# Batch 0's attention masks move from TensorE to VectorE, the mask table becomes the second transfer, and the planner gets step durations read from a trace

## The chip, the core and the metric

The kernel runs on one core of one Trainium2 chip. The metric is the device time of one execution in microseconds, lower is better. Before the change the median of three runs is 916.32 us (913.51 to 917.98).

A core has five engines, each with its own in-order queue: TensorE (PE, matmuls, with PEld for its weight loads), VectorE (DVE), ScalarE (ACT), GpSimd (POOL) and SyncE (SP), which here only issues transfers. An instruction at the head of a queue that waits holds everything behind it on that engine.

## What is computed

Attention with two kinds of sliding window, followed by a feed-forward layer with a rational activation. The masks are the part that the change is about:

```python
scores = scale * np.matmul(q, k.transpose(0, 1, 3, 2))      # 8 batches, 8 heads, 576 positions, 64 wide
mask_plain = (rel >= 0) & (rel < window)                     # window 32
mask_dil = (rel >= 0) & (rel < window * dilation) & (rel % dilation == 0)   # dilation 4
scores = np.where(masks[None, :, :, :], scores, -1000000000.0)
attn = softmax(scores)                                       # max, exp, sum, division
x = matmul(attn, v)                                          # 4608 tokens of 512
h = x @ w_in                                                 # 512 -> 2048
P = a[0] + a[1] * h + a[2] * h2 + a[3] * h3
Q = 1.0 + np.abs(b[0]) * np.abs(h) + np.abs(b[1]) * h2
out = (P / (Q + 1e-06)) @ w_out                              # 2048 -> 512
```

Heads 0 to 3 use the plain window, heads 4 to 7 the dilated one; the tokens of the dilated heads are reordered on the host so that their window is also 32 neighbours.

## The kernel before

**Attention in units.** Each batch has six units (class `Unit`). A unit is one 128 x 384 block of scores in PSUM (two banks of 192 columns), held as 32 queries by 64 keys, so each score block covers the whole window of its queries. The steps of a unit are planned in `Unit.plan` (L509): load queries and keys in one 448 KB transfer (`load_qk`), load the values in 384 KB (`load_v`), scores (`scores`, 48 small matmuls), mask, row maximum, subtraction, exponential, sum, reciprocal (VectorE and ScalarE), scaling by the reciprocal (GpSimd, `norm`), a transposition, the product with the values (`av`) and the split of the result into a high and a low part (`evac_hi`, `evac_lo`), which together are the tokens `x` of that batch. For batches 0 and 1 the transposition is done by TensorE; for the others by VectorE with a trip through DRAM. Leftover tokens (positions 512 to 575) are put aside in DRAM (`put_left`).

**The masks.** The table `mask_t` has six 64-column blocks of zeros and -1e30 in bf16, loaded once (96 KB, L903). Units of batches 0 and 1 (`on_pe`, L260) have them added by TensorE: `scores` first multiplies an identity with the mask blocks into the two banks (two matmuls of 192 columns), and then accumulates the scores on top. The scores therefore wait for the mask table and for the identity that GpSimd makes. Units of the other batches have them added by VectorE in place after the scores (`mask`, L291): one or two `tensor_tensor` instructions, by the unit's entry in `MASK_AT`. Units 0, 4 and 5 have two pieces of 192 columns, units 1 to 3 one of 384.

**The feed-forward layer in tiles.** A tile (class `Tile`) is 512 tokens by 128 of the 2048 hidden features. There are 144: nine token groups by 16 feature blocks, in the order group 0 blocks 0 to 7, group 1 all 16, group 0 blocks 8 to 15, and then groups 2 to 8. A tile is 12 matmuls into a bank (`h`), twelve steps of the activation on ScalarE, VectorE and GpSimd, and 12 matmuls into the four output banks (`out`). Group b needs the six units of batch b; the ninth group is the leftovers. The 12 matmuls come from splitting every fp32 number into a high and a low part and taking three products.

**The weights.** 32 blocks of 512 KB (16 `wi`, 16 `wo`) are loaded and each is split on the chip (`plan_weights`, L689): scaled and shifted words (ScalarE, or ScalarE or GpSimd), joined (VectorE), a high part (any of three) and a low part (VectorE or GpSimd).

**What sets the order.** Nothing is ordered by hand. A planner (class `Plan`) runs on the host while the program is built: it simulates the engines with the durations written beside every step, always taking, among steps that can start soonest on an engine, the one of the lowest rank, and emits the instructions in that order. Where a step may run on several engines, it also picks the engine. The constants that steer it:

- the cost of each step, in nanoseconds (`op({"DVE": 470}, ...)`), and the model of transfers (`DMA_START`, `DMA_NS`, `DMA_RATE`, L86);
- `DUE`: for each batch, when its last unit is due (in tiles) and the distance between its units;
- `LATE`: for each step of a tile from the 36th on, its rank beside its tile's number;
- `SLACK`: how far ahead of need scores, loads and weights (`wi`, `wo`) are ranked. For the first 36 tiles and for attention the rank of a step is worked back from the steps that need it (`Plan.due`, L106): the rank of the next step, less the cost, less the slack.

The loads of batch 0 and of the weights are chained in the order of their ranks (L980). Extra order is given with `follows`: here L909, where the mask table follows the six coefficients of the activation (`lc`). All transfers are issued by SyncE from one queue through `load` (L208). Matmuls are issued through `mm` (L211), VectorE's two-operand instructions through `tt` (L217) and `stt` (L220), GpSimd's through `ptt` (L223), ScalarE's through `act` (L214); the profile's lines are mostly those of these helpers, so tiles are named by their tensors: `pair`, `pair_A`, `pair_B` are attention's PSUM banks, `h` and `out` those of the tiles, `mx` the maxima, `p` the exponentials, `a`, `r`, `t`, `gh`, `gl` the activation's, `wi_raw` a loaded weight block, `left<-l` a store of leftovers.

Of the kernel before, what the change touches and what calls it, by code (L numbers as in the profile page):

```python
# [13 lines left out]
AF = mybir.ActivationFunctionType  # L14
# [27 lines left out]
LOG_SHIFT = 40  # L42
# [36 lines left out]
class Plan:  # L79
# [6 lines left out]
    DMA_START, DMA_NS, DMA_RATE = 3300.0, 1750.0, 375.0  # L86
# [97 lines left out]
def tile_attention_moe(  # L184
# [72 lines left out]
    class Unit:  # L257
        def __init__(self, b, u):
            self.b, self.u, self.n = b, u, b * NU + u
            self.start, self.on_pe, self.by_pe = b == 0, b < ON_PE, b < BY_PE  # L260
# [248 lines left out]
        def plan(self, by, tags):  # L509
# [20 lines left out]
            if kind == 2:  # L530
                mx = op({"DVE": 470}, 0, lambda e: self.max(True), ma)
                sb = op({"PE": 760}, 0, lambda e: self.sub_pe(), mx, identity)
                su = ex = op({"ACT": 480}, 0, lambda e: self.exp_s(), sb)
                sm = op({"DVE": 470}, 0, lambda e: self.sum(), ex)
# [3 lines left out]
            else:  # L538
                mx = op({"DVE": 470}, 0, lambda e: self.max(), ma)
                su = op({"DVE": 500}, 0, lambda e: self.sub(), mx)  # L540
                ex = op({"ACT": 425}, 0, lambda e: self.exp(), su)
                sm = op({"DVE": 470}, 0, lambda e: self.sum(), ex)
# [36 lines left out]
            if start:  # L579
                av = op({"PE": 1500}, 0, lambda e: self.av(), *self.placed, lv)  # L580
# [5 lines left out]
        def finish(self, av):  # L586
# [10 lines left out]
            low = {"DVE": sum(120 + 2 * c[1] / 0.96 for c, _ in main)}  # L597
            kl = lf = None
            if start:
                ms = eh  # L600
                if LESS[u]:
                    ms = op({"PE": sum(60 + 2 * c[1] / 1.6 for c, _ in main)}, 0, lambda e: self.less_hi(), eh, identity)
# [8 lines left out]
            else:  # L611
                low["POOL"] = sum(100 + 2 * c[1] / 0.49 for c, _ in main)
# [305 lines left out]
    for key in keys:  # L918
        plan_weights(key)
# [127 lines left out]
```

## Time and profile before

| | before |
|---|---|
| median of three runs | 916.32 us (913.51 to 917.98) |
| profiled execution | 916.49 us |
| its span in the profile | 914.7 us |
| TensorE busy | 883.2 us (97%) |
| VectorE busy | 742.3 us (81%) |
| ScalarE busy | 675.4 us (74%) |
| GpSimd busy | 467.7 us (51%) |
| mean granted TensorE clock | 0.994 of full |
| bytes moved by transfers | 103.46 MB, mean 113 GB/s |

The profile is of one execution; its own time is 916.49 us, 1.8 us more than the span from its first to its last instruction. Busy time says how long an engine was executing, not that it sets the end: TensorE's busy share is the highest, so the idle time of TensorE, stage by stage, is what can be won. "Releaser" is what ended a wait. A time to landing is from the issue of a transfer to its completion.

### The profile page before, as it was taken

Reading aid. Unit: us, or ns where it says so; the run is one execution under the profiler, and the core shown is the slowest. Engines: PE = TensorE matmul, PEld = TensorE weight load, DVE = VectorE, ACT = ScalarE, POOL = GpSimd, SP = SyncE. Lnnn points to the kernel's source line nnn. Section 1 sums busy time; section 2 is a strip of 40 time slices with the busy share of each in tenths; the row PEclk is TensorE's granted clock in tenths of the full one; section 3 lists DMA queues with packets and bytes.
Section 4 is the critical chain, followed back from the end, with each engine's and each line's share of the span. In section 5 each row is a group of like instructions: output and inputs, shape, how many; then the busy total and the mean of one; then the engine's idle time right before and its main releaser. Section 6 shows DMA issues by size and latency. Waiting matters only on the chain.

```text
span 914.7 us, 21129 instructions
## 1 busy us (share of the span) xinstructions
PE 883.2 (97%) x8153; PEld 716.1 (78%) x8153; DVE 742.3 (81%) x1312; ACT 675.4 (74%) x1092; POOL 467.7 (51%) x408
## 2 busy tenths in 40 slices
PE   5877999999999999999999999999999999999998
PEld 3755787887877878888888888888888788888876
DVE  4789999999988988788978888887779677566656
ACT  2676888877666777877787778677777688778764
POOL 2454554656635554555455555546455545444442
PEclk9989999999999999999999999999999999999999
DMA  9667460235633343334334324423333220001001
GB/s 359 240 221 249 154 234 1 99 124 190 198 99 110 110 134 118 119 111 125 115 113 127 121 83 146 129 82 85 115 95 91 61 69 1 1 1 47 0 1 47
DMA packets 85477, 103.46 MB, mean 113 GB/s; under 512 B 37376, under 2 KB 62848, under 8 KB 85376
## 3 DMA queue, kind: packets, MB, share of 16 engines
q1 hardware_dynamic: 85376, 102.11, 34.5%
q8 instruction: 64, 1.05, 0.5%
q14 instruction: 37, 0.30, 0.1%
HBM read 75.21 MB, written 26.87 MB: 112 GB/s over the span
## 4 chain that ended last, share of the span: by engine, by line
PE 75%; DVE 11%; DMA 5%; ACT 5%; issue 3%; POOL 1%; SPq 1%; DVEq 0%; POOLq 0%; ACTq 0%
PE out L212 34%; PE h L212 34%; PE pair L212 5%; DVE h L221 3%; DVE a L221 2%; DMA wi_raw<-in_w_in_dram 2%; ACT r L215 2%; DVE t L218 1%; DVE a L218 1%; DVE gl L218 1%; DMA wo_raw<-in_w_out_dram 1%; SPq L209 1%; DMA qk<-in_qk_dram 1%; ACT a L215 1%; PE pair_B L212 1%
## 5 line engine op out<-in xcount | busy, mean ns | idle before, releaser
L212 PE MATMUL h<-xh,wi 128*128 128x512 f32 x1136 | 378.1, 394 | 6.8 <-DVE a L221 6.5
L212 PE MATMUL out<-gh,wo 128*128 128x512 f32 x1136 | 353.8, 393 | 0.7 <-DVE os L218 0.7
L224 POOL TENSOR_TENSOR a<-r,a 128x512 f32<-128x512 f32 x121 | 156.6, 1294 | 241.1 <-ACT r L215 233.4
L212 PEld LDWEIGHTS h<-xh,wi 128*128 128x128 f32 x1136 | 214.5, 189 | 58.3 <-DVE a L221 12.6
L212 PEld LDWEIGHTS out<-gh,wo 128*128 128x128 f32 x1136 | 211.2, 188 | 45.9 <-DVE os L218 1.1
L212 PE MATMUL out<-gl,wo 128*128 128x512 f32 x568 | 221.8, 391 | 1.6 <-DVE gl L218 1.0
L212 PE MATMUL h<-xl,wi 128*128 128x512 f32 x568 | 222.4, 391 | 0.0
L224 POOL TENSOR_TENSOR gl<-a,gh 128x512 fp32r<-128x512 f32 x129 | 175.1, 1357 | 64.7 <-ACT gh L215 64.0
L221 DVE SCALAR_TENSOR_TENSOR h<-h,na_t,r 128x512 f32<-128x512 f32 x142 | 106.9, 753 | 111.0 <-ACT r L215 109.2
L215 ACT ACTIVATE r<-a,ln_bias 128x512 f32<-128x512 f32 x141 | 101.9, 723 | 82.8 <-POOL a L224 80.3
L215 ACT ACTIVATE r<-a,ab_t 128x512 f32<-128x512 f32 x141 | 114.7, 814 | 16.3 <-DVE a L221 14.5
L212 PEld LDWEIGHTS out<-gl,wo 128*128 128x128 f32 x568 | 106.6, 188 | 25.6 <-POOL gl L224 1.5
L212 PEld LDWEIGHTS h<-xl,wi 128*128 128x128 f32 x568 | 107.3, 189 | 21.5
L215 ACT ACTIVATE a<-h 128x512 f32<-128x512 f32 x140 | 83.5, 596 | 53.7 <-PE h L212 35.0
L215 ACT ACTIVATE t<-h,na_t 128x512 f32<-128x512 f32 x142 | 109.6, 772 | 5.0 <-PE h L212 4.6
L221 DVE SCALAR_TENSOR_TENSOR h<-t,na_t,h 128x512 f32<-128x512 f32 x142 | 107.3, 756 | 4.9
L215 ACT ACTIVATE r<-r,exp_bias 128x512 f32<-128x512 f32 x144 | 104.3, 724 | 4.7
L218 DVE TENSOR_TENSOR t<-t,h 128x512 f32<-128x512 f32 x142 | 96.6, 681 | 7.2 <-ACT t L215 7.1
L221 DVE SCALAR_TENSOR_TENSOR a<-a,r 128x512 f32<-128x512 f32 x141 | 100.2, 711 | 0.0
L221 DVE SCALAR_TENSOR_TENSOR a<-a,h 128x512 f32<-128x512 f32 x140 | 96.2, 687 | 4.8
L215 ACT ACTIVATE gh<-a 128x512 fp32r<-128x512 f32 x130 | 81.5, 627 | 23.2 <-PE out L212 14.9
L224 POOL TENSOR_TENSOR p<-p,sm 128x384 f32<-128x384 f32 x48 | 47.7, 993 | 34.3 <-DVE sm L352 28.1
(115 smaller groups left out, 712.4 us busy)
## 6 DMA issues: line engine op xcount, KB each, us to landing
qk<-in_qk_dram SPq DMA_DIRECT2D x48, 448.0 KB, 5.0
v<-in_vp_dram SPq DMA_DIRECT2D x48, 384.0 KB, 3.7
out_dram<-os SPq DMA_DIRECT2D x36, 256.0 KB, 2.3
wi_raw<-in_w_in_dram SPq DMA_DIRECT2D x16, 512.0 KB, 6.1
wo_raw<-in_w_out_dram SPq DMA_DIRECT2D x16, 512.0 KB, 6.9
results<-y SPq DMA_DIRECT2D x42, 192.0 KB, 2.4
z<-results SPq DMA_DIRECT2D x168, 48.0 KB, 2.5
turned<-u SPq DMA_DIRECT2D x36, 192.0 KB, 2.0
```

The costliest lines, as they stand in the source:

```text
L209: pin(nc.sync.dma_start(dst, src))
L212: pin(nc.tensor.matmul(o, lhs, rhs, start=start, stop=stop, skip_group_check=free))
L215: pin(nc.scalar.activation(o, i, func, **kw))
L218: pin(nc.vector.tensor_tensor(o, x, y, op))
L221: pin(nc.vector.scalar_tensor_tensor(o, x, s, y, op0, op1))
L224: pin(nc.gpsimd.tensor_tensor(o, x, y, op))
```

## The change

VectorE adds the masks of batch 0 after the scores, as it already does for batches 2 to 7; only batch 1 is left on TensorE. The mask table's load now follows the first load of unit 0 (its queries and keys), and the coefficients, unit 0's values and unit 1's queries follow the mask table. The coefficients no longer go ahead of the mask. The planner's costs are replaced by others, most of them higher, its model of transfers starts earlier (1000 instead of 3300 ns), and `DUE`, `LATE` and `SLACK` have other values, so that the order of instructions on all engines can differ everywhere.

```diff
-DUE = [(-41.16, 11.47), (-146.25, 19.43), (423.68, 72.57), (61.95, 5.87), (470.95, -17.55), (494.47, -17.25), (93.76, -24.29), (711.56, 21.96)]
+DUE = [(-42.07, 2.46), (-139.34, 32.05), (537.93, 65.82), (48.88, 1.36), (612.07, -16.51), (466.6, 3.64), (193.6, -47.08), (642.51, 32.87)]
-LATE = {"ab": -187.16, "ql": -342.11, "pl": -25.5, "qq": -118.36, "t1": -2.55, "t2": -120.77, "ln": 177.41, "ex": -496.7, "g0": -73.65, "g1": -54.63, "g2": -312.0, "gh": -189.38, "gl": 379.92, "out": 3.83}
-SLACK = {"sc": 2.49, "qk0": -51.8, "v0": -50.12, "load": 7.26, "wi": 11.43, "wo": -2.45, "w": -16.22, "gl": -5.19, "out": -6.13}
+LATE = {"ab": -175.8, "ql": -427.82, "pl": 40.09, "qq": -63.71, "t1": -55.04, "t2": 2.39, "ln": 298.24, "ex": -490.51, "g0": -123.79, "g1": -68.03, "g2": -457.35, "gh": -55.8, "gl": 283.1, "out": 3.9}
+SLACK = {"sc": 2.19, "qk0": -56.0, "v0": -56.99, "load": -3.78, "wi": 3.42, "wo": -2.73, "w": -16.4, "gl": -6.19, "out": -2.25}
...
-    DMA_START, DMA_NS, DMA_RATE = 3300.0, 1750.0, 375.0
+    DMA_START, DMA_NS, DMA_RATE = 1000.0, 1700.0, 380.0
...
-            self.start, self.on_pe, self.by_pe = b == 0, b < ON_PE, b < BY_PE
+            self.start, self.on_pe, self.by_pe = b == 0, b == 1, b < BY_PE
...
-                sc = op({"PE": 1320 + 300 * self.on_pe}, 0, lambda e: (prev.av(), self.scores()), *prev.placed, prev.lv, lq, *masks)
+                sc = op({"PE": 1320 + 700 * self.on_pe}, 0, lambda e: (prev.av(), self.scores()), *prev.placed, prev.lv, lq, *masks)
...
-                sc = op({"PE": 1130 + 320 * self.on_pe}, 0, lambda e: self.scores(), lq, *masks)
+                sc = op({"PE": 1500 + 450 * self.on_pe}, 0, lambda e: self.scores(), lq, *masks)
...
-            no = op({"POOL": 790}, 0, lambda e: self.norm(e), rc)
+            no = op({"POOL": 880}, 0, lambda e: self.norm(e), rc)
...
-                tr = op({"PE": 690}, 0, lambda e: self.transposes(), no, identity)
+                tr = op({"PE": 900 if start else 600}, 0, lambda e: self.transposes(), no, identity)
...
-                av = op({"PE": 1500}, 0, lambda e: self.av(), *self.placed, lv)
+                av = op({"PE": 2000}, 0, lambda e: self.av(), *self.placed, lv)
...
-            jn = op({"DVE": 680}, 0, lambda e: w_join(key), sc, lw, lock=True)
+            jn = op({"DVE": 710}, 0, lambda e: w_join(key), sc, lw, lock=True)
...
-        lo = op({"DVE": 602, "POOL": 1280}, 0, lambda e: w_lo(key, e), hi, lock=True)
+        lo = op({"DVE": 625, "POOL": 1350}, 0, lambda e: w_lo(key, e), hi, lock=True)
...
-    lc = op({"SP": 60}, -39.5, lambda e: load(coef_t, coef), dma=3000)
-    masked.follows.append(lc)
+    lc = op({"SP": 430}, -39.3, lambda e: load(coef_t, coef), dma=3000)
...
+    masked.follows.append(first_loads[0])
+    for o in (lc, *first_loads[1:3]):
+        o.follows.append(masked)
```

Some more costs change in the same way, nearly all upwards (the sum goes from 470 to 510, the logarithm from 615 to 660; the transposition of batch 1 goes from 690 to 600).

More of the change, by code (lines that the diff above doesn't have):

```diff
@@ L531, in plan @@
                 mx = op({"DVE": 470}, 0, lambda e: self.max(True), ma)
-                sb = op({"PE": 760}, 0, lambda e: self.sub_pe(), mx, identity)
+                sb = op({"PE": 950}, 0, lambda e: self.sub_pe(), mx, identity)
                 su = ex = op({"ACT": 480}, 0, lambda e: self.exp_s(), sb)
-                sm = op({"DVE": 470}, 0, lambda e: self.sum(), ex)
+                sm = op({"DVE": 510}, 0, lambda e: self.sum(), ex)
             elif kind:
@@ L540, in plan @@
                 su = op({"DVE": 500}, 0, lambda e: self.sub(), mx)
-                ex = op({"ACT": 425}, 0, lambda e: self.exp(), su)
-                sm = op({"DVE": 470}, 0, lambda e: self.sum(), ex)
+                ex = op({"ACT": 470}, 0, lambda e: self.exp(), su)
+                sm = op({"DVE": 510}, 0, lambda e: self.sum(), ex)
             rc = op({"DVE": 300}, 0, lambda e: self.recip(), sm)
-            no = op({"POOL": 790}, 0, lambda e: self.norm(e), rc)
+            no = op({"POOL": 880}, 0, lambda e: self.norm(e), rc)
             if self.by_pe:
-                tr = op({"PE": 690}, 0, lambda e: self.transposes(), no, identity)
+                tr = op({"PE": 900 if start else 600}, 0, lambda e: self.transposes(), no, identity)
                 pl = op(BOTH, 0, lambda e: self.place(e), tr)
@@ L596, in finish @@
             eh = op({"ACT": sum(172 + 2 * c[1] / 1.4 * 0.75 for c, _ in main)}, 0, lambda e: self.evac_hi(), got)
-            low = {"DVE": sum(120 + 2 * c[1] / 0.96 for c, _ in main)}
+            low = {"DVE": sum(200 + 2 * c[1] / 0.9 for c, _ in main)}
             kl = lf = None
@@ L601, in finish @@
                 if LESS[u]:
-                    ms = op({"PE": sum(60 + 2 * c[1] / 1.6 for c, _ in main)}, 0, lambda e: self.less_hi(), eh, identity)
+                    ms = op({"PE": sum(150 + 2 * c[1] / 1.4 for c, _ in main)}, 0, lambda e: self.less_hi(), eh, identity)
                     ms.slack = 0.0
@@ L611, in finish @@
             else:
-                low["POOL"] = sum(100 + 2 * c[1] / 0.49 for c, _ in main)
+                low["POOL"] = sum(130 + 2 * c[1] / 0.45 for c, _ in main)
                 el = op(low, 0, lambda e: self.evac_lo(e), eh, lock=True)
@@ L700, in plan_weights @@
             steps = [op({"DVE": 335}, 0, lambda e: w_copy(key), f)]
-        hi = op({"ACT": 550, "DVE": 460, "POOL": 620}, 0, lambda e: w_hi(key, e), steps[-1], lock=True)
-        lo = op({"DVE": 602, "POOL": 1280}, 0, lambda e: w_lo(key, e), hi, lock=True)
+        hi = op({"ACT": 550, "DVE": 460, "POOL": 680}, 0, lambda e: w_hi(key, e), steps[-1], lock=True)
+        lo = op({"DVE": 625, "POOL": 1350}, 0, lambda e: w_lo(key, e), hi, lock=True)
         plan.takes(steps[0], "stage", STAGE, [lo])
@@ L781, in plan @@
             Tile.last_h = h
[L782 removed]
+            ab = op({"ACT": 515}, k + LATE["ab"], lambda e: self.abs(), h)
             ql = op({"ACT": 710}, k + LATE["ql"], lambda e: self.q_lin(), ab)
@@ L793, in plan @@
             g0 = op({"DVE": 663}, k + LATE["g0"], lambda e: stt(self.ps, self.ps, na_t[:, 0:1], self.r, ALU.add, ALU.mult), ex, t2)
-            g1 = op({"DVE": 602}, k + LATE["g1"], lambda e: stt(self.a, self.a, GUARD, self.r, ALU.add, ALU.mult), ex, lock=True)
+            g1 = op({"DVE": 640}, k + LATE["g1"], lambda e: stt(self.a, self.a, GUARD, self.r, ALU.add, ALU.mult), ex, lock=True)
             g2 = op({"DVE": 602}, k + LATE["g2"], lambda e: stt(self.a, self.a, -2.0, self.ps, ALU.add, ALU.mult), g0, g1)
```

5 lines of the change are left out of this document (2 added, 3 removed).

## The prediction

> **What bounds the kernel now.** I read the busy time by stage first, to find where TensorE stands still.
>
> ```profile
> 0.00:8.00 8.00, 0.69 (x26) 0.49 (x34) 0.17 (x1) 1.49 (x2) 1.71 (x12) 1.00 0.77 269
> 8.00:20.00 12.00, 9.82 (x318) 6.93 (x306) 8.59 (x21) 4.24 (x8) 3.14 (x4) 1.00 1.03 409
> 20.00:42.00 22.00, 18.51 (x512) 15.66 (x506) 16.47 (x42) 13.00 (x43) 9.87 (x12) 1.00 0.66 234
> 42.00:69.00 27.00, 21.74 (x364) 16.96 (x365) 23.33 (x49) 19.68 (x35) 13.10 (x13) 0.87 0.73 248
> 69.00:92.00 23.00, 17.53 (x163) 13.40 (x162) 21.41 (x36) 15.98 (x28) 9.20 (x12) 0.96 0.70 242
> ...
> 180.00:260.00 80.00, 78.88 (x886) 63.35 (x886) 74.11 (x140) 59.35 (x99) 45.93 (x43) 1.00 0.50 157
> 260.00:880.00 620.00, 618.83 (x5243) 505.75 (x5242) 492.47 (x862) 467.26 (x733) 323.44 (x267) 1.00 0.29 88
> 880.00:914.70 34.70, 30.66 (x134) 24.71 (x133) 20.74 (x30) 18.98 (x28) 11.42 (x9) 1.00 0.08 31
> ```
>
> The columns are stage, length, busy time of TensorE, weight loads, VectorE, ScalarE and GpSimd (instructions in brackets), granted TensorE clock, share and rate of the transfers. From 260 to 880 us TensorE is busy 618.83 of 620 us: whatever happens there, no more than 1.17 us can be won. The idle time lies in front: 7.31 us before 8 us, 12 - 9.82 = 2.18, 22 - 18.51 = 3.49, 27 - 21.74 = 5.26 and 23 - 17.53 = 5.47 in the next four stages, and 34.70 - 30.66 = 4.04 in the tail. From 42 to 92 us the idle time is 10.73 us, and there the clock is also lowered. VectorE is the busiest engine of those two stages (23.33 of 27, 21.41 of 23), while in the first 42 us it is busy only 25.2.
>
> Next the first microseconds: SyncE's queue with the times from issue to landing, then TensorE and VectorE.
>
> ```profile
> 0.72 0.38 SPq L209 DMA_DIRECT2D qk<-in_qk_dram  x1
> ```
> ```profile
> 2.57 0.43 SPq L209 DMA_DIRECT2D mask_t<-in_mask_dram  x1
> ```
> ```profile
> qk<-in_qk_dram SPq DMA_DIRECT2D x1, 448.0 KB, 3.2
> ```
> ```profile
> mask_t<-in_mask_dram SPq DMA_DIRECT2D x1, 96.0 KB, 4.7
> ```
> ```profile
> 7.31 0.48 PE L212 MATMUL pair_A<-mask_t,ident_b 128*128 128x192 bf16 x2 [7.31 <-DMA mask_t<-in_mask_dram]
> 7.72 0.97 PE L212 MATMUL pair_A<-qk 64*32 64x64 f32 x48
> 8.73 0.56 DVE L312 TENSOR_REDUCE mx<-pair_A 128x6 f32<-128x384 f32 x1 [1.43 <-PE pair_A L212]
> ```
>
> The landing time of 3.2 us is that of the first transfer alone (the view was cut to the first issue). So unit 0's queries and keys are there at 0.72 + 3.2 = 3.92 us, and TensorE still stands until 7.31, for the masks, which were issued fifth and landed 4.7 us later (2.57 + 4.7 = 7.27). That wait is real and the change takes it away.
>
> Then the chain of waits and the waits of TensorE from 30 to 120 us.
>
> ```profile
> 7.77 9.45 DMA wi_raw<-in_w_in_dram
> ...
> 24.04 1.22 PE pair L212 x50
> ...
> 37.37 6.17 DMA wi_raw<-in_w_in_dram
> ...
> 89.19 4.61 PE h L212 x12
> ...
> 216.77 2.72 PE h L212 x12
> ```
> ```profile
> PE h L212 <- DVE a L221: 5.7, 3, 3.4
> PE pair L212 <- DVE mx L312: 2.6, 2, 1.5
> PE pair L212 <- ACT p L215: 2.6, 2, 2.5
> PE out L212 <- DVE gl L218: 1.0, 1, 1.0
> ```
>
> The early chain goes through transfers of weights (9.45 and 6.17 us), and the twelve matmuls of a tile take 4.61 us after a stand where they take 2.72 otherwise. No wait of TensorE in this list is for a weight: tiles wait for VectorE's last product of an older tile (5.7 us), attention for row maxima and exponentials.
>
> **The change part by part.** The profiled execution took 916.49 us (span 914.7 and 1.8 around it), the median of the runs is 916.32; the sum is made against 916.5.
>
> *Mask second.* Scores of unit 0 no longer need the mask or the identity. They start when the queries are in, 3.92 + 0.04 (the step from 7.27 to 7.31) = 3.96. VectorE came 8.73 - 7.72 = 1.01 us after the scores' start, so the mask add starts at 4.97. The mask, 96 KB right behind 448 KB, must land by then: its bytes at 269 GB/s take 0.37 us, so about 4.3 us. The cost of the add comes from the later batches, where VectorE does it already:
>
> ```profile
> L218 DVE TENSOR_TENSOR pair<-pair,mask_t 128x192 f32<-128x192 f32 x36 | 13.0, 362 | 0.8
> ...
> L218 DVE TENSOR_TENSOR pair<-pair,mask_t 128x384 f32<-128x384 f32 x18 | 10.0, 556 | 0.0
> ```
>
> Unit 0 has two pieces, 2 x 0.362 = 0.72, so its first maximum begins at 5.69 instead of 8.73: a lead of 3.04 us. The lower end: if the mask again takes 4.7 us from an issue at 1.16, it lands at 5.86, the maximum begins at 6.58 and the lead is 2.15.
>
> *Masks of the other five units.* TensorE loses a pair of mask matmuls per unit, which held the scores back by 7.72 - 7.31 = 0.41 us; VectorE gains 0.56 or 0.72 us between scores and maximum. Net 0.15 to 0.31 us per unit. In the chain up to 42 us only one further set of scores of batch 0 stands (the piece at 24.04, unit 5, two pieces), so I charge 0.31 once. Over the batch VectorE gains 3 x 0.556 + 6 x 0.362 = 3.84 us. What hides it is VectorE's idle time before 42 us, 42 - 25.2 = 16.8 us. If that cover is gone (rival 1) it costs 3.84 minus the lead, 0.8. What queues behind a mask add on VectorE is its own unit's maximum and the previous unit's sums; GpSimd's scaling waits for those and TensorE's transposes for it.
>
> *Order of the loads.* Due times of batch 0 now lie 2.46 apart instead of 11.47. A load's rank is the due time behind it, less the costs of the steps between (each plus 150 ns, in tiles of 4743 ns), less the slacks, and the lower rank goes first. By hand: for unit 5's queries -42.07 - 3.3 - 2.19 + 56.0 = 8.4, for wi block 0 0 - 1.4 - 3.42 + 16.4 = 11.6; before, -41.16 - 2.9 - 2.49 + 51.8 = 5.3 and 0 - 1.4 - 11.43 + 16.22 = 3.4. So unit 5's queries move ahead of the first wi block, and early queries go ahead of older units' values. The coefficients now go behind the mask, and behind no unit but 0. So wi block 0 goes to the queue behind one more 448 KB: at the 409 GB/s of 8 to 20 us that is 1.1 us later. It stands in the chain (the 9.45 us piece), so the ends for what the lead is worth are a loss of 1.1 and a gain of 3.04. I take the lead whole, 3.04 - 0.31 = 2.7, because the piece after that transfer is ScalarE converting weights ahead of an output copy of unit 0, an order that the plan can choose otherwise when the unit is 3 us earlier.
>
> *New durations and due times.* They touch no instruction, only order and the choice of engine, so their worth has no row of its own. The place where a truer plan can help is 20 to 92 us:
>
> ```profile
> 17.23 2.72 SPq L209 DMA_DIRECT2D v<-in_vp_dram  x3
> 27.40 3.42 SPq L209 DMA_DIRECT2D left<-l  x2
> ```
> ```profile
> 30.00:32.00 2.00, 2.00 (x71) 1.47 (x70) 1.54 (x6) 0.91 (x5) 0.13 (x1) 1.00 0.09 8
> ```
>
> SyncE issues nothing from 19.95 to 27.40 because the store of leftover tokens waits at its head; the rate then falls from the 409 GB/s of 8 to 20 us to 8 GB/s and the weight load of the chain goes out only at 37.37. ScalarE holds its queue for that load with an exponential of batch 1 behind it. Of TensorE's stands I credit the new plan with the one for ScalarE's exponentials (2.6) and the one for a product on VectorE (1.0), 3.6 us. Ends: at the top all 10.73 us of idle time from 42 to 92, plus the lost clock, 0.13 x 27 + 0.04 x 23 = 4.4, together 15.1; at the bottom a loss as long as the 7.45 us stand, should the new order make another one.
>
> *The long middle.* New priorities of the tiles' steps (the linear term after the attention instead of before it, the second product behind the first) reorder ScalarE and VectorE. I take 0. Ends: a gain of 1.17, and a loss of 8.7 us if the middle stood as the stage before it does (1.12 of 80, times 620). The tail of 4.04 us I leave.
>
> Sum: 916.5 - 2.7 - 3.6 = 910.2 us.
>
> *A rule that speaks against the change.* The first rows of scores are slow, and get quick at about 35 us:
>
> ```profile
> 30.64 0.97 PE L212 MATMUL pair<-qk 64*32 64x64 f32 x48
> ...
> 32.97 1.65 PE L212 MATMUL pair<-mx,ident 128*128 128x192 f32 x4
> ...
> 35.80 0.72 PE L212 MATMUL pair<-qk 64*32 64x64 f32 x48
> ```
>
> The granted clock reads 1.00 there, but 48 scores took 0.97 us at 30.64 and 0.72 at 35.80, after the dense matmuls at 32.97. Dense mask matmuls are what the change takes out of batch 0, so this is rival 4. The Trainium skill (TensorE: Matmul & The Clock Gate, Part 1) says that idleness throttles TensorE and some 3.4 us of sustained activity release it. By that rule alone the scores at 30.64, long after the first matmul, should have been fast; the trace does not bear that out, so small matmuls seem to count for little, and I leave the sum as it is.
>
> **The rivals.**
>
> 1. *VectorE or the transfers swallow the lead.* The lead of 3.04 is eaten by VectorE's 3.84 us of adds, or ends at the wi block that lands 1.1 us later, and the plan's credit does not come. For it: VectorE is busy 23.33 of 27 and 21.41 of 23 us from 42 to 92. Against: nearly 17 us of idle VectorE before. Time: 916.5 - 3.04 + 3.84 = 917.3 to 916.5 - 2.7 = 913.8, about 915.5. This is also the case in which the new durations do not do what they are said to.
>
> 2. *Weights come late: slower.* The wi blocks' slack falls from 11.43 to 3.42 tiles, and 8.01 x 4.743 = 38 us of the plan's lead for their splitting goes. One mechanism, at tiles 1 to 8 (now 54 to 92 us): SyncE stands again, as for 7.45 us, with a wi block behind it, and a tile of TensorE stands for the block. Price 7.45, and 4.61 - 2.72 = 1.9 for a tile at a lowered clock, less the lead of 2.7: 916.5 + 6.65 = 923.2. It decides once a block lands after TensorE is free for it. For it: the fall to 8 GB/s. Against: no tile waits for a weight now.
>
> 3. *The plan closes most of the early gaps.* Of 10.73 us of stands and 4.4 of clock two thirds go, 10.1, with the lead 12.8: 903.7. For it: stands have different causes and all lie in the stretch that the durations describe. Against: VectorE is at 93% from 69 to 92 us.
>
> 4. *The clock is released later.* Without the mask matmuls two more units run slow: scores lose 0.97 - 0.72 = 0.25 us each, and if every small matmul of a unit (scores, product with the values, transposes) loses in that proportion, about 1.2 us per unit: 910.2 + 2.4 = 912.6.
>
> **How the numbers follow.** The forecast gets 0.40, rival 3 gets 0.11, rival 1 0.27, rival 4 0.03 and rival 2 0.19. A difference of 0.5% is 4.6 us, about what a measurement of this kernel can tell from no change; faster means below 911.7 us, slower above 920.9. The forecast and rival 3 are faster: 0.51. Rivals 1 and 4 lie within: 0.30. Rival 2 is slower: 0.19. The range runs from 900 (rival 3 and some of the top end of the plan's credit) to 922 (just short of rival 2's price); beyond lie about 0.06 below and 0.13 above. The likeliest case alone has 906 to 911.7.
>
> **What would show it.** Right for the start: the first scores near 4.0 us, the mask landed before 4.9, the first mask add near 5.0, the first maximum near 5.7. Right for the loads: queries of unit 5 before the first wi block. Right for the plan: SyncE's longest stand before 45 us well under 7.45 us, no fall to 8 GB/s, the idle time of TensorE from 42 to 92 below 8 us. Right for the middle: still within about 1 us of full. Wrong would be: TensorE tiles waiting for a weight's split (rival 2), VectorE above 90% before 42 us with the first tile no earlier than 41.9 us (rival 1), or idle time in the middle, which the sum does not have at all.

## The result, and the profile after

The changed kernel takes 921.28 us (median of 17 runs, 918.86 to 927.95), the kernel before beside it on the same chip 915.56 us (17 runs, 913.51 to 918.58). The ratio is 1.0073, 95% interval 1.0057 to 1.0089: slower by 0.7%, 5.7 us, where 6.3 us less had been forecast. The time lies inside the predicted range, on the side that had been given 0.19, and 0.7 us from its upper end. One run of a later experiment (e17) took 2206.95 us, far from its ten others; the ratio leaves it out. The profiled execution, 918.86 us with a span of 916.7, is the fastest of the seventeen, and its span is only 2.0 us longer than that of the kernel before, so its trace holds the smaller part of the loss.

The busy time by stage of the changed kernel (stage, length, busy time of TensorE, weight loads, VectorE, ScalarE, GpSimd, granted TensorE clock, share and rate of the transfers):

```profile
0.00:8.00 8.00, 1.95 (x98) 1.50 (x99) 2.15 (x6) 1.82 (x3) 1.71 (x12) 1.00 0.74 252
8.00:20.00 12.00, 8.33 (x249) 6.42 (x249) 10.67 (x28) 3.83 (x8) 4.07 (x5) 1.00 1.03 407
20.00:42.00 22.00, 17.49 (x447) 14.34 (x448) 16.27 (x37) 17.18 (x54) 11.60 (x14) 1.00 0.92 336
42.00:69.00 27.00, 19.12 (x393) 14.29 (x369) 19.53 (x39) 13.23 (x23) 13.23 (x13) 0.89 0.57 177
69.00:92.00 23.00, 20.23 (x267) 15.18 (x265) 20.76 (x40) 17.61 (x31) 11.36 (x12) 0.95 0.73 240
...
260.00:880.00 620.00, 619.82 (x5246) 505.80 (x5245) 485.19 (x860) 467.44 (x731) 331.57 (x279) 1.00 0.29 90
```

TensorE stands 6.05 us before 8 us (7.31 before the change), then 3.67 and 4.51 up to 42 us (2.18 and 3.49), 7.88 and 2.77 up to 92 us (5.26 and 5.47). So the start wins 1.3 us and the next 34 us lose 2.5; the stretch from 42 to 92 us, from which 3.6 us were to come, stands 10.65 us against 10.73; from 92 to 180 us it stands 2.48 us against 1.49. The middle is as full as before.

Start of the changed kernel: two transfers (KB, time from issue to landing), then TensorE's and VectorE's first instructions.

```profile
mask_t<-in_mask_dram SPq DMA_DIRECT2D x1, 96.0 KB, 3.0
coef_t<-in_coef_dram SPq DMA_DIRECT2D x1, 3.0 KB, 3.9
```
```profile
3.99 0.97 PE L212 MATMUL pair_A<-qk 64*32 64x64 f32 x48 [3.99 <-DMA qk<-in_qk_dram]
```
```profile
5.59 0.17 DVE L889 TENSOR_SCALAR na_t<-coef_t 128x4 f32<-128x4 f32 x1 [5.59 <-DMA coef_t<-in_coef_dram]
5.68 0.77 DVE L218 TENSOR_TENSOR pair_A<-pair_A,mask_t 128x192 f32<-128x192 f32 x2
6.48 0.56 DVE L312 TENSOR_REDUCE mx<-pair_A 128x6 f32<-128x384 f32 x1
```

The scores start at 3.99 us and the mask is there at 1.16 + 3.0 = 4.2. But VectorE's queue has another instruction ahead of the mask: the coefficients' change of sign, which waits for a 3 KB transfer until 5.59. The first maximum begins at 6.48 us, 2.25 us earlier than before.

That lead is 2.46 us at the scores of the first unit of batch 1 (28.18 us, before 30.64) and 0.36 at the next (35.44, before 35.80). At the first matmul of the first tile it is a loss of 0.50 us (before, then changed):

```profile
41.89 0.50 PE L212 MATMUL h<-xh,wi 128*128 128x512 f32 x1
```
```profile
42.39 0.50 PE L212 MATMUL h<-xh,wi 128*128 128x512 f32 x1
```

The chain of waits of the changed kernel says what these microseconds hang on (start, length, what):

```profile
2.57 5.29 DMA qk<-in_qk_dram
...
7.87 9.10 DMA v<-in_vp_dram
...
16.99 8.77 DMA wi_raw<-in_w_in_dram
...
25.78 0.74 ACT wi_raw L215
26.53 0.33 ACT xh L215 x2
...
32.40 0.67 ACT wo_f L663
33.07 0.70 ACT xh L215 x2
33.81 0.76 PE pair_B L212 x2
```

From 2.57 to 25.78 us the chain is transfers and nothing else, queries, values and a weight block, each released by the one before it. From 8 to 20 us they move 407 GB/s with all 16 transfer engines busy (share 1.03). In this trace no compute engine stands in the chain there. Then ScalarE holds a copy of an attention output (`xh`) behind the conversion of a weight block, here a `wo` block that the new order has among the first `wi` blocks.

The largest new wait stands at 60 to 67 us. Waits of TensorE from 30 to 120 us (us in total, times, longest), and then the rows of SyncE, ScalarE and TensorE around it:

```profile
PE pair L212 <- ACT p L215: 5.0, 2, 4.1
PE h L212 <- DVE a L221: 2.7, 4, 1.1
PE pair L212 <- DVE mx L312: 2.1, 1, 2.1
PE pair L212 <- DVE p L218: 2.0, 1, 2.0
PE pair_B L212 <- ACT xh L215: 1.6, 1, 1.6
```
```profile
53.94 5.75 SPq L209 DMA_DIRECT2D qk<-in_qk_dram  x2
59.91 1.88 SPq L209 DMA_DIRECT2D z<-results  x4
```
```profile
64.41 0.52 ACT L215 ACTIVATE xh<-z 128x384 fp32r<-128x384 f32 x1 [4.51 <-DMA z<-results]
```
```profile
66.73 0.97 PE L212 MATMUL pair<-v,pT 64*32 64x64 f32 x48 [4.12 <-ACT p L215]
```

The second of the two query loads at 53.94 is unit 12's. Its buffer comes free only with the scores of an older unit, and so SyncE stands 4.9 us for TensorE with the four `z` reads behind it; ScalarE stands 4.51 us for `z` with the exponential of the next unit behind that, and TensorE stands 4.12 us for the exponential. In the kernel before the same four reads went out at 54.55 us:

```profile
54.55 1.74 SPq L209 DMA_DIRECT2D z<-results  x4
```

The planner had not ordered that. In its plan the reads of `z` and then the values of unit 10 come ahead of unit 12's queries. The helper that keeps the planned order ties an instruction only to the one directly ahead of it on its engine; at this place the freeing of the first PSUM pool (L871) puts untied instructions on the queue between the values and the queries, and the query load slid forward past both of these loads. It is the only such slip of the changed kernel, and the kernel before has none.

### The profile page after: what moved, and what is told of

Read it like the earlier page. It is cut to its first block, busy times and chain, and to the rows that moved or that the text cites. A ratio compares the mean times of both kernels' runs of the same rounds, so it can differ in the third digit from the quotient of the medians.

```text
span 916.7 us, 21155 instructions
## 1 busy us (share of the span) xinstructions
PE 883.8 (96%) x8141; PEld 716.0 (78%) x8141; DVE 736.0 (80%) x1307; ACT 676.7 (74%) x1094; POOL 479.4 (52%) x420
## 4 chain that ended last, share of the span: by engine, by line
PE 70%; DVE 12%; DMA 8%; ACT 4%; issue 2%; SPq 2%; POOL 1%; DVEq 0%; ACTq 0%; POOLq 0%
PE h L212 34%; PE out L212 32%; PE pair L212 4%; DVE a L221 3%; DVE h L221 3%; DMA z<-results 2%; ACT r L215 2%; SPq L209 2%; DMA results<-y 1%; DMA wi_raw<-in_w_in_dram 1%; DMA v<-in_vp_dram 1%; DVE t L218 1%; DVE a L218 1%; POOL a L224 1%; ACT xh L215 1%
## 5 line engine op out<-in xcount | busy, mean ns | idle before, releaser
L224 POOL TENSOR_TENSOR a<-r,a 128x512 f32<-128x512 f32 x122 | 158.9, 1302 | 253.7 <-ACT r L215 234.5
L224 POOL TENSOR_TENSOR gl<-a,gh 128x512 fp32r<-128x512 f32 x135 | 181.7, 1346 | 54.2 <-ACT gh L215 47.6
L224 POOL TENSOR_TENSOR p<-p,sm 128x384 f32<-128x384 f32 x48 | 45.7, 953 | 25.5 <-DVE sm L352 20.9
```

The costliest lines, as they stand in the source:

```text
L224: pin(nc.gpsimd.tensor_tensor(o, x, y, op))
```

## Experiments

All ratios are to the kernel before, run on the same chip beside it. "Pinned" is a kernel in which every instruction is also tied to the program's own latest one on its engine; on the kernel before that moves nothing. "The planner's own end" is the time at which the planner's simulation ends while the program is built; it is 907.3 us for the kernel before and 909.9 for the changed one, which is by its own reckoning 2.7 us longer.

### The transfer out of order

e1 is the changed kernel with the tie:

```diff
-    pin = tc.keep_in_program_order
+    newest = {}
+    def pin(ins):
+        tc.keep_in_program_order(ins)
+        before = newest.get(ins.ins.engine)
+        if before is not None:
+            tc.add_manual_dep(ins.ins, before, ..., reason="program order")
+        newest[ins.ins.engine] = ins.ins.name
+        return ins
```

> The changed kernel with one transfer moved: queries of unit 12 go out behind, not ahead of, the four loads of unit 7's results (z7) and the values of unit 10, where the planner had put them; every other instruction keeps its place on its engine. Theory Q (that one place in SyncE's queue is the loss): the stand of 4.12 us of TensorE near 62 us goes, z7 is issued near 55 instead of 59.9 us, the time falls by 3.5 to 4.5 us from 921.3 to about 917, level with before within 2 us. Theory V (VectorE's added work or the new order as a whole is the loss): the stand moves elsewhere and the time stays at 920 to 922.

918.81 us (12 runs), ratio 1.0033 [1.0022, 1.0043]. The `z` reads of e1, and TensorE's wait for the exponential from 30 to 120 us:

```profile
58.00 1.73 SPq L218 DMA_DIRECT2D z<-results  x4
```
```profile
PE pair L221 <- ACT p L224: 1.1, 1, 1.1
```

The slip costs 1.0073 - 1.0033 = 0.4%, some 2.5 us by the medians, and the wait of 5.0 us is down to 1.1. Part of it moved: in e1 the wait for a subtraction on VectorE is 3.6 us, in the changed kernel 2.0. In the stretch from 42 to 92 us of e1,

```profile
42.00:69.00 27.00, 23.17 (x457) 17.08 (x446) 22.22 (x45) 15.35 (x31) 13.43 (x13) 0.87 0.68 210
69.00:92.00 23.00, 18.67 (x257) 13.82 (x256) 19.15 (x39) 17.29 (x31) 11.77 (x11) 0.90 0.70 230
```

TensorE stands 3.83 + 4.33 = 8.16 us, where in the changed kernel it stands 10.65. A third of a per cent is left.

e6 is the changed kernel once more, with nothing edited.

> The changed kernel as it is, beside the others on one chip, for its time and a second trace. Theory Q: again the stand near 62 us for z7, 920 to 922, 2.5 to 3.7 us above the pinned kernel.

921.04 us, ratio 1.0065 [1.0041, 1.0089]. In its trace the stand is longer still:

```profile
54.07 7.81 SPq L209 DMA_DIRECT2D qk<-in_qk_dram  x2
```
```profile
PE pair L212 <- ACT p L215: 5.3, 2, 4.7
```

### One part alone, planned anew

e2: all of the changed kernel, pinned, but batch 0's masks on TensorE as before.

```diff
-            self.start, self.on_pe, self.by_pe = b == 0, b == 1, b < BY_PE
+            self.start, self.on_pe, self.by_pe = b == 0, b < ON_PE, b < BY_PE
```

> The changed kernel with the transfer put right as in the run before, and batch 0's masks on TensorE again; the mask stays the second transfer, and all planner numbers stay the new ones. Theory V: VectorE's 3.8 us of mask adds were the loss, so this is faster than the run before by 1 to 4 us. Theory Q: the adds are hidden, the planner makes another order, and the time lies within 3 us of the run before on either side.

933.64 us, ratio 1.0192 [1.0177, 1.0206].

e4: the reverse edit in the kernel before, and the mask table as the second transfer; due times and durations of before.

```diff
-            self.start, self.on_pe, self.by_pe = b == 0, b < ON_PE, b < BY_PE
+            self.start, self.on_pe, self.by_pe = b == 0, b == 1, b < BY_PE
...
-    masked.follows.append(lc)
+    masked.follows.append(first_loads[0])
+    for o in (lc, *first_loads[1:3]):
+        o.follows.append(masked)
```

> The kernel before with only the masks of batch 0 on VectorE and the mask table second, with all planner numbers as before. Theory N (the new planner numbers lose what the mechanical part wins): 2 to 4 us faster than before, 912 to 914. Theory V: 0 to 4 us slower than before. If the lead simply dies in the waits behind it: within 1.5 us of before.

930.30 us, ratio 1.0138 [1.0121, 1.0155]; TensorE's tiles stand for VectorE over the whole execution (before: 6.5 us in 5 stands):

```profile
PE h L221 <- DVE a L230: 15.6, 15, 3.5
```

e7: the kernel before with the new `DUE`, `LATE` and `SLACK` alone. e8: the kernel before with the new durations and transfer model alone (the diffs are those lines of the change).

> The kernel before with only the due times, LATE and SLACK of the change; masks, loads and durations as before. Theory P (due times fit one set of durations and steps, and the end that the planner itself works out says what the chip will do, about 9 us more): its plan ends at 915.1 us, 7.9 later than that of the kernel before, so 924. Theory that the new due times are better as such: faster than before.

> The kernel before with only the new durations and the new model of transfers; masks, loads and due times as before. Theory P: its plan ends at 921.7 us, so about 930.5 on the chip. Theory that truer durations make a better order as such: no slower than before.

e7 took 924.72 us, ratio 1.0095 [1.0064, 1.0127], and e8 930.74, 1.0161 [1.0129, 1.0193]. So by the medians e2, e4, e7 and e8 are all slower than the whole change. That doesn't price the parts: due times are fitted to one set of steps and durations, and with anything else the planner makes another order on every engine. Up to here the times also followed the planner's own end plus 9 us, all but e2 (930.6 + 3.0). The runs with new due times below take that rule back.

### What the lead at the start is worth

e3: pinned, and the coefficients' change of sign is issued behind unit 0's subtraction, so that the first mask waits for nothing.

```diff
         def sub(self):
+            if self.n == 0:
+                pin(nc.vector.tensor_scalar(na_t, coef_t[:, 0:4], -1.0, None, ALU.mult))
...
-        pin(nc.vector.tensor_scalar(na_t, coef_t[:, 0:4], -1.0, None, ALU.mult))
```

> The changed kernel with the transfer put right, and VectorE's scaling of the coefficients emitted behind unit 0's subtraction instead of ahead of its mask add; nothing else moves. The mask add of unit 0 now starts near 5.0 instead of 5.68 us. If the start's lead reaches the end, the time falls by 0.6 us against the pinned kernel; if the lead dies before the first tile (theory D), it does not change beyond 0.5 us.

917.75 us, ratio 1.0023 [1.0011, 1.0035], beside 1.0033 [1.0022, 1.0043] for e1: the intervals overlap, nothing is settled. In e1's own trace the coefficients happened to land at 4.43 us, so there was little to win.

e5: pinned, and ScalarE's conversion of the `wo` block is put behind unit 4's output copies (the wait of 1.65 us of the chain above).

```diff
+            if self.n == 4:
+                w_scale(held.pop())
...
+    held = [("wo", 1)]
     def w_scale(key):
+        if key in held:
+            return
```

> The changed kernel with the transfer put right, and on ScalarE the conversion of one weight block (wo 1), which stands at 31 us for a staging buffer, moved behind the copies of unit 4's result that stood behind it. Nothing else moves. Theory D (the start's lead dies in that wait): TensorE's wait of 1.65 us near 32 us goes, batch 1's second unit and the first tile come 1.5 us earlier, and 1 to 1.5 us of it reach the end: 917 to 917.5 where the pinned kernel has 918.8. Rival (what follows waits for something else anyway): the wait goes and the time stays within 0.5 us of the pinned kernel.

919.77 us, ratio 1.0033 [1.0020, 1.0047], no gain. The stand moved on to the next weight: from e5's chain of waits, and from the rows of ScalarE and TensorE,

```profile
31.29 8.88 DMA wo_raw<-in_w_out_dram
```
```profile
40.20 0.74 ACT L224 ACTIVATE wo_raw<-wo_raw,low_bias 128x512 int32<-128x512 uint32 x1 [2.00 <-DMA wo_raw<-in_w_out_dram]
```
```profile
42.90 0.93 PE L221 MATMUL pair_A<-xh,minus 128*128 128x64 f32 x3 [3.97 <-ACT xh L224]
```

the block that ScalarE next converts lands 8.88 us after its issue, and an attention copy stands behind it.

e9: pinned, and the mask table and the coefficients are issued behind unit 3's queries; all else keeps its place.

```diff
             load(t, qk[self.n])
+            if self.n == 3:
+                load(coef_t, coef)
+                load(mask_t, mask)
...
-    masked = op({"SP": 430}, -39.4, lambda e: load(mask_t, mask), dma=P * 768)
+    masked = op({"SP": 430}, -39.4, lambda e: None, dma=P * 768)
...
-    lc = op({"SP": 430}, -39.3, lambda e: load(coef_t, coef), dma=3000)
+    lc = op({"SP": 430}, -39.3, lambda e: None, dma=3000)
```

> The pinned changed kernel (that of e1), with one edit: the mask table and the coefficients are issued behind the queries of unit 3 instead of right behind those of unit 0. All else stays in its place. The first mask add should begin near 7.6 us instead of 5.68, so the lead of the first maximum over the kernel before falls from 2.25 us to about 0.3. Theory L (the lead at the start is worth what it measures): 918.8 + 1.9 = 920.7 us, ratio to before near 1.0054. Theory Q (the lead is dead by the first tile, because ScalarE's queue of weight conversions and the weight transfers set when unit 4's tokens are ready): 918.8 within 0.5 us, ratio 1.0028 to 1.0038, and the first tile within 0.5 us of 42.4.

The edit did more than it was meant to: behind 2.2 MB the mask landed late, and the first maximum of e9 began at 11.89 us (first row), where that of e1 began at 5.86 (second row).

```profile
11.89 0.56 DVE L324 TENSOR_REDUCE mx<-pair_A 128x6 f32<-128x384 f32 x1
```
```profile
5.86 0.56 DVE L321 TENSOR_REDUCE mx<-pair_A 128x6 f32<-128x384 f32 x1
```

With 6 us lost at the start the time is 921.43 us, ratio 1.0056 [1.0036, 1.0077]: 2.6 us more than e1 by the medians, though the two intervals overlap. The first tile of e9 starts at 47.10 us, that of e1 at 43.80. So of a loss twice as large as the lead about half arrives at the first tile and, by the medians, less than half at the end.

### New due times

The due times decide the order, so the parts were also compared with `DUE`, `LATE` and `SLACK` fitted to each set of steps: values for which the planner's own end came earliest, found from different starts. All are pinned. Their edits are these three lines and, where batch 0's masks move in a kernel with the durations of before, that of e4; shown are the three lines of e12, and e11 has the same numbers in full precision. e10 and e16 have the steps and durations of before, e11 and e15 have the masks on VectorE, the mask table second and the durations of before, e13 has all of the change, durations too.

```diff
-DUE = [(-41.16, 11.47), (-146.25, 19.43), (423.68, 72.57), (61.95, 5.87), (470.95, -17.55), (494.47, -17.25), (93.76, -24.29), (711.56, 21.96)]
+DUE = [(-39.49, 2.58), (2.63, 111.83), (670.02, -18.51), (229.95, -26.72), (425.31, 56.88), (633.81, 33.88), (514.99, 87.59), (574.22, 95.86)]
...
-LATE = {"ab": -187.16, "ql": -342.11, "pl": -25.5, "qq": -118.36, "t1": -2.55, "t2": -120.77, "ln": 177.41, "ex": -496.7, "g0": -73.65, "g1": -54.63, "g2": -312.0, "gh": -189.38, "gl": 379.92, "out": 3.83}
-SLACK = {"sc": 2.49, "qk0": -51.8, "v0": -50.12, "load": 7.26, "wi": 11.43, "wo": -2.45, "w": -16.22, "gl": -5.19, "out": -6.13}
+LATE = {'ab': 122.28, 'ql': -602.34, 'pl': 1110.83, 'qq': -790.21, 't1': 679.05, 't2': -2431.9, 'ln': -1764.11, 'ex': -656.93, 'g0': -479.76, 'g1': -525.24, 'g2': -427.33, 'gh': -1247.95, 'gl': 654.82, 'out': 3.74}
+SLACK = {'sc': 1.72, 'qk0': -50.74, 'v0': -63.51, 'load': 92.85, 'wi': 3.45, 'wo': -2.68, 'w': -22.94, 'gl': -7.84, 'out': -3.04}
```

> The kernel before, with its own masks, durations and transfer model, and other due times: a set for which the planner's own end is 903.9 us instead of 907.3 (and the tie that keeps the transfers in planned order). Theory P (the chip's time follows the planner's own end, plus about 9 us): 912.9 us, ratio 0.9964, faster than both kernels. The rival (the order of the plan is worth what the start of the attention is worth, and the due times of before were already the best for this start): 916 us, ratio 1.000 within 0.1%.

> The masks of batch 0 on VectorE and the mask table as second transfer, with the durations of before and due times fitted to this set of steps: the planner's own end is 907.2 us. Theory P: 907.2 + 9 = 916.2 us, ratio 1.000, that is 14 us less than the same steps with the due times of before (930.3), and no better than the kernel before. Theory M (moving the masks itself costs time by VectorE's 3.84 us more, whatever the plan): 920 us or more, ratio 1.0042.

> The kernel of e11 with its due times rounded to two decimals and nothing else; the planner's own end goes from 907.2 to 922.6 us by that alone. Theory P: 922.6 + 9 = 931.6 us. If the numbers are only a means and the order hardly changes the time: within 2 us of e11.

> The changed kernel with its masks, its load order, its durations and its transfer model, and other due times, fitted to them; the planner's own end is 908.4 us (909.9 with the change's own). Theory D (the new durations, most of them raised, are what misleads the plan): no better than the pinned changed kernel, 917 to 920 us, ratio 1.002 to 1.004. Theory N (only the due times given with the change fit badly): as e11, about 912 us, ratio 0.996.

> The masks on VectorE and the mask table as second transfer in the kernel before, its durations kept, and a second set of due times, found independently of that of e11; the planner's own end is 907.6 us. Theory S (moving the masks is worth its time wherever the due times fit it): 911 to 914 us, ratio 0.995 to 0.998. Theory U (e11 is the luck of one set of numbers; the plan's end says nothing closer than 5 us): anything from 911 to 921, most likely 916.

> The kernel before with its masks on TensorE and a second set of fitted due times, found independently of that of e10; the planner's own end is 904.2 us. Theory S: the masks on TensorE keep the start late, so 915 to 918 us as in e10, ratio 0.999 to 1.003. Theory U: anything from 909 to 919.

| run | steps, durations | planner's own end, us | time, us (runs) | ratio |
|---|---|---|---|---|
| e10 | before, before | 903.9 | 917.07 (12) | 1.0006 [0.9991, 1.0020] |
| e16 | before, before | 904.2 | 916.05 (10) | 1.0007 [0.9992, 1.0023] |
| e11 | masks moved, before | 907.2 | 911.37 (5) | 0.9950 [0.9934, 0.9967] |
| e15 | masks moved, before | 907.6 | 919.14 (6) | 1.0034 [1.0018, 1.0050] |
| e12 | e11, rounded to two decimals | 922.6 | 925.52 (2) | 1.0101 [1.0076, 1.0127] |
| e13 | masks moved, new | 908.4 | 916.06 (10) | 1.0005 [0.9992, 1.0017] |

The rule of the planner's end plus 9 us falls: the difference goes from 2.9 us (e12) to 13.2 (e10). The plan is right to some 5 us either way, more than any part of the change is worth. Refitted, the new durations are neither better nor worse than the old ones (e13). The moved masks come out at 911 us in one fit and at 919 in the other, so no single fit says what moving them is worth, and e11 owes its time at least in part to its particular order. It is faster than both kernels all the same. That rounding the numbers costs 14 us shows how loosely they hold that order.

e14 takes e11 and issues mask table and coefficients behind unit 2's queries (the edit of e9, with a 2 for the 3).

> The kernel of e11 with the mask table and the coefficients issued behind the queries of unit 2, all else in its place. The first maximum should begin about 1.5 to 2.5 us later, near 8.5 us, as in the kernel before. Theory L (the lead at the start is what e11 gains): the time goes up by as much, to 913 to 914 us, ratio 0.9975. Theory Q (the lead is lost before the first tile): 911.4 within 0.7 us.

The first maximum of e14 (first row) begins 3.2 us after that of e11 (second row), and later than that of the kernel before (8.73):

```profile
9.07 0.56 DVE L324 TENSOR_REDUCE mx<-pair_A 128x6 f32<-128x384 f32 x1
```
```profile
5.84 0.56 DVE L321 TENSOR_REDUCE mx<-pair_A 128x6 f32<-128x384 f32 x1
```

e14 takes 910.36 us (4 runs), ratio 0.9938 [0.9918, 0.9957], beside 0.9950 [0.9934, 0.9967]. The first tile of e14 starts at 39.49 us, that of e11 at 39.28. So in e11's order 3.2 us less at the start are 0.2 us at the first tile and no time at the end, although in e14's trace the chain from 8 to 19 us goes through VectorE. By the medians it is the shortest time of this case.

### The masks alone, in an unchanged order

e17 (from e11) and e18 (from e1) move batch 0's masks back to TensorE without planning anew: the additions on VectorE for the six units go, mask matmuls go ahead of each unit's scores, and every other instruction keeps its place.

```diff
         def scores(self):
-            on_pe = self.on_pe
+            on_pe = self.b < 2
...
         def mask(self):
+            if self.start:
+                return
```

> The kernel of e11 with one edit that doesn't plan anew: batch 0's six mask additions on VectorE are left out, and each unit's scores are preceded by the two mask matmuls on TensorE instead, as in the kernel before; every other instruction keeps its place on its engine. TensorE gains 6 x 0.41 = 2.5 us before 42 us and VectorE loses 3.84 us. Theory M (the moved masks are what makes 911 us): back by the start's and the units' share, 913.5 to 916 us, ratio 0.998 to 1.000. Theory O (only the order matters; where the masks are added is hidden by idle time on both engines): 911 us within 1 us, ratio 0.994 to 0.996.

> The same edit in the pinned changed kernel (that of e1), without planning anew: batch 0's masks back on TensorE, every other instruction in its place. Theory M: 918.8 plus 2 to 4 us, 921 to 923 us, ratio 1.0055 to 1.0075. Theory O: 918.8 us within 1 us, ratio 1.002 to 1.0045, although the same masks with a plan of their own took 933.6 us in e2.

e17 takes 914.93 us, ratio 0.9983 [0.9972, 0.9994]: in e11's order the masks on VectorE are worth 0.33%. e18 takes 916.53 us, ratio 0.9997 [0.9983, 1.0011]: in the changed kernel's order they cost 0.36%, against both expectations. The granted clock hardly explains e17's loss, though its row reads 0.69 from 20 to 42 us and that of e11 reads 1.00. At 28 us the same scores take as long in e17 (second row) as in e11 (third row), and at 20.61 us e17 has quicker ones (first row):

```profile
20.61 0.72 PE L221 MATMUL pair<-qk 64*32 64x64 f32 x48
```
```profile
28.17 0.97 PE L221 MATMUL pair<-qk 64*32 64x64 f32 x48
```
```profile
28.22 0.97 PE L221 MATMUL pair<-qk 64*32 64x64 f32 x48
```

Why the 1.00 of e11 is not to be read as a fast clock is told in the last section.

e18 also says where the early maximum comes from. Its masks are on TensorE, the mask table is second, and VectorE's first maximum begins at

```profile
5.71 0.56 DVE L323 TENSOR_REDUCE mx<-pair_A 128x6 f32<-128x384 f32 x1 [1.10 <-PE pair_A L221]
```

as early as in e1 (5.86). In this order the whole lead of the first maximum is the place of the transfer; moving the additions has no share in it.

The traces of e1 and e18 part company at three places. The scores of the second unit of batch 1 start at 36.71 us in e1 and at 35.87 in e18. TensorE's clock first goes to full at 43.2 us in e1 and at 39.5 in e18 (see the last section). And a write of 192 KB to DRAM, which a read follows and then two weight loads, lands late in e1. The issue and its median time to landing, in e1 and then in e18, and the transfers of e1 after the bulk of that write (111 to 112.6 us):

```profile
turned<-u SPq DMA_DIRECT2D x1, 192.0 KB, 3.8
```
```profile
turned<-u SPq DMA_DIRECT2D x1, 192.0 KB, 2.0
```
```profile
DMA packets 17, 0.01 MB, mean 8 GB/s; under 512 B 1, under 2 KB 17, under 8 KB 17
```

Some 15 us later TensorE stands 2.08 us for a product on VectorE in e1 (at 126.31 us) and 0.21 us in e18 (at 121.60); that the late write leads to this stand was not followed step by step. In the traces of the changed kernel, unedited, the same write lands after 2.3 us. So the late write came with the tie, and left with the masks: the step from the changed kernel to e1 may hide a part of what the slip costs, and the step from e1 to e18 may hold something that isn't the additions' own.

e1's profiled execution, 921.23 us, is the slowest of its twelve, so the two traces differ by more than the medians do, and of each kernel there is one.

## Why the prediction was wrong, step by step

**The sum of the 0.73%, by runs that don't plan anew.** Changed kernel 1.0073; its transfer put in order, 1.0033; its masks back on TensorE, 0.9997. So 0.40% is the slip, for which the sum had no term, 0.36% is what comes with the moved masks in this order, and the new due times and durations, with the mask table second, come to nothing: e18 is as fast as the kernel before. Each difference is uncertain by about 0.2%, and how the late write divides between the first two is open.

**"New durations and due times: 3.6" failed.** It was the largest term. I picked two stands out of the trace and credited the new plan with removing them. The stand for ScalarE's exponential went from 2.6 to 5.0 us, since the new order stumbled over a load; without the slip it is 1.1 (e1), so 1.5 of those 2.6 us were there to be had, and the stand for the product (1.0) did go. But other stands came in their place, 2.0 us for a subtraction on VectorE and 1.6 for `xh`, and from 42 to 92 us 10.65 us of standing are left of 10.73. A list of stands shows what is late in one order; in a new order other things are late. That the new plan is by its own reckoning 2.7 us longer could have been had from the diff, by carrying out the planner's simulation, though only as a hint, since that reckoning is off by 5 us either way; I had costed single ranks by hand. The bottom end of this term, another stand as long as 7.45 us, is what happened: one of 4.9 us.

**"I take the lead whole, 2.7" failed.** The mechanism at the very start was right: scores at 3.99 us (3.96 predicted), mask at 4.2 (4.3). The lead was 2.25 us instead of 3.04, because VectorE's queue also held the coefficients, which the change puts behind the mask: I named what a mask add holds up, and not what stands ahead of it. In other executions the coefficients come in time (4.43 us in e1). Moving them out of the way showed nothing clear in the time (e3). What failed is that the lead was passed on: 2.25 us at the first maximum are a loss of 0.50 us at the first tile. In the trace the chain up to 25.78 us is transfers, and behind them copies wait on ScalarE for converted weights. My own reservation, that the 9.45 us transfer stands in the chain, was the better half of that paragraph. e14 takes 3.2 us of lead away and loses nothing, but in e11's order; in the order of the change e9 passes on about half of a larger loss, so what the 2.25 us are worth there was not measured by itself.

**"0.31 for the other units, VectorE's 3.84 us hidden" is unsettled.** The masks alone cost 0.36% in one order and gain 0.33% in another. The cover of 16.8 us of idle time was an average: from 8 to 20 us VectorE is busy 10.67 of 12 us in the changed kernel, 8.59 before. How much of e18's gain is these additions, how much the late write of e1 and how much its late clock is not told apart.

**"Unit 5's queries ahead of the first wi block" was right** in order, and worth nothing. SyncE's longest stand before 45 us fell from 7.45 us to 27.05 - 21.89 = 5.2, and the rate from 20 to 42 us rose from 234 to 336 GB/s, as the sign for the plan demanded; yet no gain. The fall to 8 GB/s came at 58 to 60 us instead, in the stand with unit 12's queries. e11 stands longer still, from 16.5 to 24.6 us, and is faster, so the length of such a stand alone decides nothing.

**The middle at 0 was right**: 0.18 us of standing, 1.17 before. The idle time from 42 to 92 us, which was to fall below 8 us, did not.

**The rivals.** Rival 2 had the side and nearly the size (923.2 us), and one half of its mechanism: SyncE stood 4.9 us. But what stood behind it was a read of `z`, not a weight, and no tile waited for a weight; that its price (7.45 + 1.9 us, less the lead of 2.7) comes near is luck. Rival 1 has half of its sign: the first tile is no earlier than 41.9 us (42.39), but VectorE is busy 29.1 of the 42 us before it, not above 90%; the time worked out for it was 915.5. Rival 4 is in the trace. In the changed kernel the slow matmuls last one unit longer:

```profile
35.44 0.97 PE L212 MATMUL pair<-qk 64*32 64x64 f32 x48
36.34 1.51 PE L212 MATMUL pair_A<-pT,v 64*64 64x32 f32 x48
37.78 0.90 PE L361 MATMUL t<-ident,p 128*128 128x128 f32 x3
38.48 1.21 PE L212 MATMUL pair<-mx,ident 128*128 128x192 f32 x4
...
41.73 0.72 PE L212 MATMUL pair<-qk 64*32 64x64 f32 x48
```

In the kernel before the same four, from 35.80 us on, take 0.72, 0.90, 0.55 and 0.82 us: 2.99 us against 4.59 here. That is 1.6 us of TensorE's time, for which the rival had 1.2 per unit and the sum nothing; how much of it reaches the end is not shown. The reason given for the rival is not borne out: e18, with the mask matmuls back, shows the same 0.97 at 35.87 us, while in e17, with mask matmuls too, scores are quick at 20.61 us and slow again at 28.17.

## What to carry to other kernels

Before a lead at the start is credited, look at what the next 20 us hang on: where transfers run at full rate, an engine's lead may go no further. Where a planner orders the program, its constants belong to one set of steps; a part can only be priced in an unchanged order, and a fitted plan is worth measuring more than once, since its own end was wrong by 5 us either way while the effects sought were 3. And compare the emitted order with the planned one: one load ahead of two others cost 0.4%.

## What the hardware showed that was not expected

**A transfer waits for its last part.** The 192 KB write of e1 had moved nearly all its bytes after two of its 3.8 us; for the rest a trickle of 8 GB/s ran, 17 packets, a sixteenth of the write's 272. In the middle of it the trace has one packet of instruction loading:

```profile
q8 instruction: 1, 0.02, 8.7%
```

(from 110 to 111 us: packets, MB, share of the engines' time). The Trainium skill (DMA: Bandwidth & Descriptors, "Why a DMA increments its semaphore by 16 and not by 1") says that a transfer runs on up to 16 engines that finish independently and is complete when the last has reported. The trace agrees: the landing comes at the end of the trickle and not of the bulk. Whether the instruction packet delays the last part is open. The same write takes 3.8, 4.4 and 3.5 us in e3, e5 and e9, each with such a packet in its window, and 2.0 us in e18, without one; but in both traces of the changed kernel (the second is e6) it takes 2.3 us with such a packet near its end. No run tried it by itself.

**A granted clock of 1.00 that was none.** 48 scores take 0.97 us in the first stretch of the traces and 0.72 later: still 0.97 at 35.44 us in the changed kernel and at 36.71 in e1, where the rows read a granted clock of 1.00. Where the rows read 0.50, the same scores take 0.97 too (at 68.06 us in the changed kernel, at 28.17 in e17). The traces' records of the granted clock begin only where it first goes to full, at 35.6 us in the kernel before, 39.3 in the changed one, 43.2 in e1 and 34.2 in e11, and the rows count the time ahead of it as full clock. So until then TensorE ran as at half clock, and the rows' 1.00 is no measurement. The Trainium skill (TensorE: Matmul & The Clock Gate, Part 1) gives about 3.4 us of sustained activity until the clock is released. This doesn't fit e1, if small matmuls count as activity: TensorE is busy 6.98 of the 7 us from 36 to 43 us, and the product that starts at 41.81 us still takes 0.97 us (0.72 at 40.81 in the changed kernel). What counts as activity no run here shows.
